# Copying softmax reciprocals to all partitions: four one-row DMA transfers in place of one four-row transfer, in a planned attention and spectral-filter kernel

## The chip, the core and the metric

The kernel runs on one core of a Trainium2 chip. The core has a matrix engine (PE, "TensorE"), a vector engine (DVE), a scalar engine (ACT, which computes exponentials), a general engine (POOL, "GpSimd") and a sequencer (SP) that here issues nearly all DMA transfers. Matrix products go to PSUM banks (512 float32 columns by 128 partitions); everything else lies in SBUF (128 partitions) or in DRAM. The metric is the device time of one launch in microseconds (us), lower is better; the median of several runs counts. The profile is of one further execution.

## The reference, cut to what matters

```
x: [1, 2048, 448]   wqkv: [448, 1344]   wo: [448, 448]   16 heads of 28
q, k, v = split(x @ wqkv)
a = softmax(q k^T / sqrt(28)) v, heads joined, @ wo
b = irfft2(rfft2(x) * (w_r + i w_i))          # over positions and channels, to bf16
g = sigmoid(sum(x * gate_w))                  # one number per position
out = g * a + (1 - g) * b
```

All inputs are bf16. The large part is the softmax: 16 heads x 2048 x 2048 = 67 million exponentials.

## The kernel before, in words

**Tiling.** Heads are taken four at a time: group g (0 to 3) has four heads, each on 32 of the 128 partitions. Queries are cut into four chunks c of 512. So there are 16 rounds n = (g, c), in an order that `plan_steps` gives (line 676). In each round the 2048 keys are 16 tiles kt of 128. A unit is one head's score tile, 128 keys by 512 queries.

**Exact exponentials.** Scores go to the PSUM tiles psA (three units) and psB (two units) in turn; ACT takes the exponential of all three or two at once (line 1307) into a ring of 28 slots in SBUF. These are the 336 steps of the kernel. A product with v (`pvb<-ring,vw`) sums over keys into one PSUM bank, and the same product sums the weights, so that row 28 of each head's 32 partitions has the softmax's denominator.

**Approximated exponentials.** `ND[n]` of the 16 key tiles of a round don't go through ACT: DVE adds a constant to the score and writes it as a 16-bit integer that read as bf16 is roughly an exponential (line 1261, four per key tile), three copies shifted by a fraction of an octave are made on POOL or DVE (line 1273), and four products with v (`pvb<-pd,vd`) average the error away. Their scores go to one of two shared PSUM banks, bg.

**Background.** The same two banks also serve the projections of q and k, v, and the Fourier part. The latter has a forward half (`fwd`, `fwd2`, each tile copied by a DMA, `xtok<-Ab`), a middle half that multiplies by the weights (loads `CS` and `Wg`), and a last part of 16 tiles, for each of which SP reads `V<-xtok` and `og<-gsc`, PE multiplies (`bg<-A,V`) and DVE writes X (line 1678). Output tiles (`out_tile`, `last_tile`) add the Fourier part (`bg<-Bd,X`) and the attention part (`bg<-wo,q`) in PSUM.

**Normalisation.** At the end of a round, `normalise` (line 1396) copies the PSUM bank to pvs (DVE, line 1443), SP moves the four rows of denominators to a 128 x 16 tile (`rs<-pvs`), DVE takes reciprocals (line 1446), POOL multiplies by the gate (line 1447), SP writes them to a DRAM scratch of four rows of 512 (`rsc<-rrg`), SP copies each of the four rows to 32 partitions (`Rb<-rsc`), and POOL multiplies pvs by Rb into q's place (line 1456). The last round does this with PE and no DMA.

**What sets the order.** The program order of each engine is written out by a planner. `Sched.run` simulates the engines with a guessed duration for each operation and a guessed latency for each hand-over, takes at each moment the ready operation with the smallest key, and emits the instructions in that order. Keys are due times: of the step that needs a result, minus a lead. The engines then run in the planned order, each waiting on semaphores for what it needs, so a late transfer stops the engine that awaits it and all that is planned behind. The constants that the change touches are these. `ND` is the number of approximated key tiles per round. `LRB` and `LREM` are planned latencies of the Rb copy and of the two Fourier copies (added to an issue's duration). `TA, TB` are the time span over which the Fourier part is due, `WREL` how long before its due time its forward half may start. `FLEAD`, `XLEAD`, `QLEAD`, `WLEAD`, `PJE` and `PJV` are leads and spreads of the projections. `DUE_P`, `DHOLD`, `PLEAD`, `EL`, `ELAST` place the approximated exponentials, `PVD` their products with v, `URG` and `DUP` are priorities on PE, `SWP` a penalty for a change of PE's tiling, `RWAIT` how long PE is kept free for a score, `KO` and `KP` the delay of output tiles and the lead of the last partial sums.

```
T.append(t)                                   # plan_steps, l. 709: start of a step
t += 0.052 + 512 * len(st) / 1200.0
def due(c): return t_a + (t_b - t_a) * c / total          # background, l. 1554
d = self.dma(lambda v2=v2: v2[:], ..., vev + [v2r[t % 2]], k - 4, lat=LREM)   # V<-xtok, l. 1663
```

Of the kernel before, what the change touches and what calls it, by code (L numbers as in the profile page):

```python
# [31 lines left out]
def free_dims(ap, dims, offset=0):  # L32
    return _AP(tensor=ap.tensor, offset=ap.offset + offset,
               ap=[list(ap.ap[0])] + [list(d) for d in dims])


def rows_of(ap, row0, stride, count, dims, offset=0):
    pitch = ap.ap[0][0]
    return _AP(tensor=ap.tensor, offset=ap.offset + row0 * pitch + offset,
               ap=[[pitch * stride, count]] + [list(d) for d in dims])  # L40
# [133 lines left out]
FIRST = 0  # L174
FWANT = (0.4, 0.45, 0.5, 0.55)
HAND = 0.15
DUE_P = 4.97
SWP = 0.58
PVA, PVD = -2, 0.69
URG = 1  # L180
FLEAD = 3.91
SQPOOL = 0
EL, ELAST = 1.87, 2
NLD = 2
KP = 26.63
KN, KO, PLEAD, DSP, DHOLD, RWAIT, WREL, XLEAD, QLEAD, WLEAD = 0, 19.35, 3.2, 0.49, 6.47, 1.51, 18.58, 8.27, 12.54, 4.09
DW, DS = 0.64, 0.4
LDMA, LREM, LRB = 2.02, 3.04, 6.5
DUP = 0.55


def frees(o):
# [3 lines left out]
class Sched:  # L196
# [60 lines left out]
    def run(self, nbg_tiles, dunits, dfree):  # L257
# [94 lines left out]
        while left:  # L352
            progress = False
            for e in engs:
# [8 lines left out]
                for o in pend[e]:  # L363
# [4 lines left out]
                    if o.acq is not None:  # L368
                        bl = [b for b in range(nbg_tiles) if held[b] is None and banks[b] <= t + 1e-9]
                        if not bl:  # L370
                            continue
                        if ud is not None and o.name != "dunit" and len(bl) == 1 and ud < o.key + DUP:
                            continue
# [3 lines left out]
                    if e == "PE":  # L377
                        if o.name == "pv" and URG and any(o in exps[i].deps for i in range(nexte, nexte + URG) if i in exps):
                            k -= 60.0
                        sw = SWITCH if (mode is not None and o.mode is not None and mode != o.mode) else 0.0  # L380
                        if sw:
                            k += SWP
                        if o.name != "score" and nexts in scores:
# [141 lines left out]


class Kernel:
    ND = [0, 3, 3, 3, 3, 3, 3, 4, 3, 3, 3, 3, 3, 2, 3, 4]
    RING = 28
    T0 = 10.0  # L530
    PJE, PJV = 25.21, 16.0
    TA, TB = 46.46, 360.74

    def __init__(self, ctx, tc, A_x, A_wqkv, A_wo, w_r, w_i, gate_w, out):
        self.ctx, self.tc, self.nc = ctx, tc, tc.nc
# [139 lines left out]
    def plan_steps(self):  # L675
# [5 lines left out]
        for n, (g, c) in enumerate(self.groups):  # L681
            nd = self.ND[n]
            dk = [NT - 1 - i for i in range(nd)]
# [503 lines left out]
    def attention(self):  # L1187
# [7 lines left out]
        for b in range(4):  # L1195
            due = ts[0] + 4 * b * rate
            if b:
                self.x_block(b, due - XLEAD)
                self.proj_fast(b, due - FLEAD)
            wop = self.w_block(0, [b], due + 5.0)  # L1200
# [31 lines left out]
        for n, kt in dlist:  # L1232
# [15 lines left out]
            for s in range(4):  # L1248
                it = Item()

                def fm(s=s, g=g, c=c, kt=kt, it=it):
                    self.mm(self.bgi(it), self.k[g][32 * s:32 * s + 32, 128 * kt:128 * kt + 128],
                            self.q[g][32 * s:32 * s + 32, 512 * c:512 * c + 512], True, True, tile_position=(32 * s, 0))
                due = fdue[0] - DUE_P + DSP * s
                m = sc.op("PE", 0.22, fm, self.kev[g, kt // 4] + self.qev[g, c], due - 1, rel, "row", it, name="dunit")
# [140 lines left out]
    def normalise(self, n, last):  # L1396
        nc, sc = self.nc, self.sc
        g, c = self.groups[n]
        i = n % 2
        t0 = self.tstart[n + 1] + 2.0  # L1400
        if not hasattr(self, "nlast"):
            self.nlast, self.rblast = [None, None], None
        pvs, rs, rr, rrg = self.pvs[i], self.rs[i], self.rr[i], self.rrg[i]
        dst = self.q[g][:, 512 * c:512 * c + 512]
        if n == 15:
            kk = -50.0
            ev = []
            for h in range(2):
                ev.append(self.act(0.33, lambda h=h: self.pin(nc.scalar.copy(
                    out=pvs[:, 256 * h:256 * h + 256], in_=self.pv[:, 256 * h:256 * h + 256])),  # L1410
                    last + [self.nlast[i]] + ev, -100.0))
            sums = self.psA[:, 2, :]
            home = [self.pv[:], self.psA[:, 1, :]]
            ms = []
            for j in range(4):
                ms.append(self.pe(0, lambda j=j: self.mm(sums[:, 4 * j:4 * j + 4], pvs[:, 128 * j:128 * j + 128],
                                                         self.c("self").bitcast(F32)[:, 0:128:32], True, True),
                                  [ev[j // 2], self.lastexp[0]] + ms[-1:], kk, dur=0.25))
            r = self.rs[i]
            a = self.dve(0.2, lambda: self.pin(nc.vector.reciprocal(out=r[:], in_=sums[:, 0:16])), ms[-1:], kk)  # L1420
            self.lastrec = a
            xs = []
            for h in range(2):
                xs.append(self.dve(0.3, lambda h=h: self.pin(nc.vector.tensor_tensor(
                    out=self.Rx[:, 2 * h:2 * h + 2, :].rearrange("p j (s n) -> p j s n", n=32),
                    in0=free_dims(r[:], [[4, 2], [1, 4], [0, 32]], 8 * h),
                    in1=free_dims(self.glog[:], [[1, 2], [0, 4], [0, 32]], 12 + 2 * h), op=ALU.mult)),
                    [a, self.gate_f32, self.rblast] + xs, kk, lk=True))
            ms2 = []
            for j in range(4):  # L1430
                ms2.append(self.pe(0, lambda j=j: self.mm(home[j // 2][:, 128 * (j % 2):128 * (j % 2) + 128],
                                                          self.Rx[:, j, :], self.c("idf").bitcast(F32), True, True),
                                   [xs[j // 2]] + ev[1:] + ms2[-1:], kk, dur=0.25))
            self.onlast = []
            for j in range(2):
                self.onlast += [self.dve(0.37, lambda j=j: self.pin(nc.vector.tensor_tensor(
                    out=dst[:, 256 * j:256 * j + 256], in0=pvs[:, 256 * j:256 * j + 256],
                    in1=home[j][:, 0:256], op=ALU.mult)), [ms2[2 * j + 1], ev[1]], kk + j)] * 2
            for t in range(12, 16):
                self.last_tile(t)  # L1440
            return ev[1]
        kk = t0 + KN
        ev = self.dve(0.61, lambda: self.pin(nc.vector.tensor_copy(out=pvs[:], in_=self.pv[:])),
                      last + [self.nlast[i]], -100.0)
        d1 = self.dma(lambda: rs[:], lambda: rows_of(pvs[:], DH, 32, 4, [[16, 32], [1, 16]]), (ev,), kk)
        a = self.dve(0.16, lambda: self.pin(nc.vector.reciprocal(out=rr[:], in_=rs[:])), (d1,), kk)
        b = self.pool(0.15, lambda: self.pin(nc.gpsimd.tensor_tensor(out=rrg[:], in0=rr[:], in1=self.G4[:, c, :],
                                                                     op=ALU.mult)), [a] + self.g4d, kk)
        sc_ = self.rsc[i]
        d2 = self.dma(lambda: sc_[:].rearrange("s (r j) -> (s r) j", j=16), lambda: rrg[:], (b, self.nlast[i]), kk, dur=DS)  # L1450

        def bc():
            src = sc_[:]
            return _AP(tensor=src.tensor, offset=src.offset, ap=[[512, 4], [0, 32], [1, 512]])
        ds = [self.dma(lambda: self.Rb[:], bc, (d2, self.rblast), kk, dur=0.55, lat=LRB)]
        e = self.pool(1.15, lambda: self.pin(nc.gpsimd.tensor_tensor(out=dst, in0=pvs[:], in1=self.Rb[:], op=ALU.mult)),  # L1456
                      ds, kk)
        self.nlast[i] = self.rblast = e
        self.onorm[g, c] = e
        if g == 3:  # L1460
            for t in range(4 * c, 4 * c + 4):
                self.out_tile(t, t0 + KO)
        return ev
# [36 lines left out]
    def last_tile(self, t):  # L1500
# [7 lines left out]
        if t % 2:  # L1508
            k0 = 6
            itp = Item()  # L1510
            part = self.sq[:].bitcast(F32)[:, 512 * (i // 2):512 * (i // 2) + D]
            kp = self.tstart[16] - KP + i
            ps = []
# [216 lines left out]
```

## Time and profile before

| | |
|---|---|
| median of 3 runs | 407.27 us (407.16 to 408.46) |
| profiled execution | 407.7 us, of which the span from first to last instruction 405.9 us |
| ACT busy | 386.7 us (95%) |
| PE busy | 383.3 us (94%), mean granted clock 0.992 |
| DVE, POOL busy | 290.7 us (72%), 247.5 us (61%) |
| DMA | 20.93 MB in 30271 packets, mean 52 GB/s |
| Rb<-rsc | 15 transfers of 256 KB, issued from 57.2 to 382.7 us, 547 ns for an issue |
| V<-xtok | 16 transfers of 112.5 KB, issued from 312.2 to 364.2 us |

How to read it: a group names its line, engine and operation, then what it writes and reads (`ring<-psA`), how often it ran, the busy time of all and the mean of one, and after a second bar the engine's idle time before it with who ended it. A matmul's line is that of a helper (L669), and a DMA issue's too (L644), so those are told apart by their tiles. In a timeline a line has the start, the length, the engine and the operation, with an idle time in square brackets. The granted clock is the share of full speed that PE was given.

### The profile page before, as it was taken

What the parts mean: (1) busy time and instruction counts of PE and PEld (TensorE: products, weight loads), DVE (VectorE), ACT (ScalarE), POOL (GpSimd) and SP (SyncE); (2) the same over time, 40 slices, a digit from 0 to 9 for tenths busy, and PEclk for the clock granted to TensorE, in tenths of its full rate; (3) what the DMA queues carried; (4) which work ended last, traced back from release to release, by engine and by line L of the source; (5) the groups of instructions that cost most, each with busy time, mean ns of one, the idle gap of its engine ahead of it and who ended that gap; (6) DMA issues with size and microseconds to landing.
All of it is one profiled execution on the core that took longest, in us unless ns stands there. A gap on an engine that the chain in (4) does not pass through costs nothing.

```text
span 405.9 us, 14400 instructions
## 1 busy us (share of the span) xinstructions
PE 383.3 (94%) x6206; PEld 154.3 (38%) x6207; DVE 290.7 (72%) x502; ACT 386.7 (95%) x355; POOL 247.5 (61%) x226
## 2 busy tenths in 40 slices
PE   8999999999999999999999999999998999979996
PEld 5444333334433333333443333444343334323333
DVE  1654776788787978977889888788677567544782
ACT  3999999999999999999999999999999999988992
POOL 8811583571656579389596895677797953353310
PEclk9999999999999999999999999999999999988999
DMA  8600012100101131121211221121211122220111
GB/s 204 161 2 5 7 45 55 47 25 18 41 26 47 49 82 60 32 64 28 57 45 38 56 52 42 40 77 30 68 30 47 46 84 71 66 80 14 38 39 45
DMA packets 30271, 20.93 MB, mean 52 GB/s; under 512 B 15508, under 2 KB 28032, under 8 KB 30208
## 3 DMA queue, kind: packets, MB, share of 16 engines
q1 hardware_dynamic: 29440, 19.70, 17.6%
q8 instruction: 48, 0.79, 0.8%
q10 hardware_dynamic: 768, 0.32, 0.4%
q14 instruction: 15, 0.12, 0.1%
HBM read 14.13 MB, written 1.97 MB: 40 GB/s over the span
## 4 chain that ended last, share of the span: by engine, by line
ACT 65%; PE 21%; issue 10%; DMA 3%; DVE 0%; ACTq 0%
ACT ring L1307 65%; PE bg L669 7%; PE pvb L669 5%; PE psA L669 4%; PE psB L669 3%; DMA V<-xtok 1%; DMA xtok<-in_A_x_dram 1%; PE bg L672 1%; DVE vw L1140 0%; DVE V L1537 0%; ACT w L1089 0%; PE psB L672 0%; PE pvb L672 0%; ACT ge L1159 0%; ACTq L1307 0%
## 5 line engine op out<-in xcount | busy, mean ns | idle before, releaser
L1307 ACT ACTIVATE ring<-psA 128x1536 bf16<-128x1536 f32 x168 | 275.5, 1640 | 5.8 <-PE psA L669 5.6
L1273 POOL TENSOR_SCALAR pd<-pd 128x2048 uint16<-128x2048 uint16 x99 | 186.0, 1902 | 71.2 <-DVE pd L1261 45.3
L1307 ACT ACTIVATE ring<-psB 128x1024 bf16<-128x1024 f32 x168 | 204.3, 1216 | 0.4 <-PE bg L669 0.4
L1261 DVE TENSOR_SCALAR pd<-bg 128x512 uint16<-128x512 f32 x184 | 124.7, 686 | 40.5 <-PE bg L669 37.9
L669 PEld LDWEIGHTS <-k 32*128 32x128 bf16 x1024 | 46.7, 91 | 126.3 <-issue 118.6
L669 PE MATMUL pvb<-ring,vw 128*32 128x512 bf16 x840 | 77.9, 386 | 0.0
L669 PE MATMUL psA<-q,k 32*128 32x512 bf16 x504 | 66.8, 384 | 10.2 <-ACT ring L1307 6.9
L669 PE MATMUL bg<-q,k 32*128 32x512 bf16 x184 | 70.4, 385 | 0.0
L669 PE MATMUL psB<-q,k 32*128 32x512 bf16 x336 | 65.9, 383 | 4.2 <-ACT ring L1307 3.3
L669 PE MATMUL pvb<-pd,vd 128*32 128x512 bf16 x736 | 67.4, 384 | 0.0
L1456 POOL TENSOR_TENSOR q<-pvs,Rb 128x512 bf16<-128x512 f32 x15 | 19.1, 1274 | 22.8 <-DVE pd L1273 21.2
L669 PEld LDWEIGHTS <-vw 128*32 128x32 bf16 x840 | 20.4, 95 | 27.3 <-issue 24.1
L669 PEld LDWEIGHTS <-vd 128*32 128x32 bf16 x736 | 19.4, 95 | 20.1 <-issue 15.0
L1273 DVE TENSOR_SCALAR pd<-pd 128x2048 uint16<-128x2048 uint16 x39 | 26.5, 703 | 0.4
L669 PEld LDWEIGHTS <-xT 128*32 128x32 bf16 (+1 forms) x1280 | 20.1, 96 | 11.8 <-issue 8.9
L1629 DVE TENSOR_TENSOR t<-bg,Wg 128x450 bf16<-128x450 f32 x32 | 18.8, 617 | 4.1 <-PE bg L669 2.2
L669 PE MATMUL bg<-xT,wpq 128*32 128x512 bf16 (+2 forms) x243 | 19.2, 383 | 0.1
L669 PE MATMUL bg<-xT,wpk 128*32 128x512 bf16 (+2 forms) x244 | 18.6, 380 | 0.0
L669 PE MATMUL bg<-Bd,xT 128*32 128x450 bf16 (+1 forms) x256 | 17.5, 357 | 0.0
L669 PE MATMUL bg<-Bd,X 113*32 113x448 bf16 x240 | 17.0, 370 | 0.3 <-DVE X L1678 0.3
L669 PE MATMUL bg<-wo,q 128*32 128x448 bf16 x232 | 16.3, 363 | 0.0
L1575 DVE CAST X<-bg 128x450 bf16<-128x450 f32 x16 | 10.0, 625 | 8.7 <-PE bg L669 8.4
(119 smaller groups left out, 351.0 us busy)
## 6 DMA issues: line engine op xcount, KB each, us to landing
Rb<-rsc SPq DMA_DIRECT2D x15, 256.0 KB
CS<-cCS SPq DMA_DIRECT2D x16, 192.0 KB
xtok<-Ab SPq DMA_DIRECT2D x16, 112.5 KB
V<-xtok SPq DMA_DIRECT2D x16, 112.5 KB
xtok<-in_A_x_dram SPq DMA_DIRECT2D x4, 448.0 KB
out_dram<-fin SPq DMA_DIRECT2D x12, 112.0 KB
Wg<-in_B_w_r_dram SPq DMA_DIRECT2D x32, 28.1 KB
Wg<-in_B_w_i_dram SPq DMA_DIRECT2D x32, 28.1 KB
```

The costliest lines, as they stand in the source:

```text
L669: self.pin(self.nc.tensor.matmul(out, lhsT=lhsT, rhs=rhs, start=start, stop=stop, **kw))
L672: self.pin(self.nc.tensor.transpose(out=out, in_=in_, identity=self.c("ident")[0:n, 0:n]))
L1261: self.pin(nc.vector.tensor_scalar(out=ys[:, s, :].bitcast(U16), in0=self.bgi(it), scalar1=127 * UNITS, scalar2=0.0, op0=ALU.add, op1=ALU. ...
L1273: self.pin(e.tensor_scalar(out=fl(pds), in0=fl(ys), scalar1=float(PHASE[f]), scalar2=1.0, op0=ALU.add, op1=ALU.mult))
L1307: self.pin(nc.scalar.activation(out=self.ring[:, u0:u0 + len(st), :], in_=slot[:, 0:len(st), :], func=ACT.Exp, scale=LN2 / UNITS))
L1456: e = self.pool(1.15, lambda: self.pin(nc.gpsimd.tensor_tensor(out=dst, in0=pvs[:], in1=self.Rb[:], op=ALU.mult)), ds, kk)
L1575: x1.append(self.dve(.54, lambda: self.pin(nc.vector.tensor_copy(out=self.X1[:, t, 0:F2], in_=self.bgi(it)[:, 0:F2])), ops[-1:] + pads, k, ...
L1629: self.pin(nc.vector.tensor_tensor(out=out[:], in0=self.bgi(it)[:, 0:F2].rearrange("p (a f) -> p a f", a=2), in1=free_dims(Wg[:], [[F - 2 ...
```

## The change

The copy of the reciprocals, one DMA whose source has three dimensions (four rows, each read 32 times, 512 numbers), becomes four DMAs, one per row, each to its own 32 partitions. The planner counts each with 0.5 us of issue and the latency LRB. The multiply on POOL depends on all four. Beside it 22 constants and the list ND have new values. The rest of the planner and all arithmetic stay.

```diff
-DUE_P = 4.97
-SWP = 0.58
-PVA, PVD = -2, 0.69
-URG = 1
-FLEAD = 3.91
+DUE_P = 7.01
+SWP = 0.98
+PVA, PVD = -2, 0.64
+URG = 2
+FLEAD = 6.57
 SQPOOL = 0
-EL, ELAST = 1.87, 2
+EL, ELAST = 1.93, 2.4
 NLD = 2
-KP = 26.63
-KN, KO, PLEAD, DSP, DHOLD, RWAIT, WREL, XLEAD, QLEAD, WLEAD = 0, 19.35, 3.2, 0.49, 6.47, 1.51, 18.58, 8.27, 12.54, 4.09
+KP = 24.94
+KN, KO, PLEAD, DSP, DHOLD, RWAIT, WREL, XLEAD, QLEAD, WLEAD = 0, 20, 3.19, 0.49, 6.56, 1.49, 4, 8.32, 16.29, 5.66
 DW, DS = 0.64, 0.4
-LDMA, LREM, LRB = 2.02, 3.04, 6.5
-DUP = 0.55
+LDMA, LREM, LRB = 2.02, 3.0, 3.16
+DUP = -1.85
...
-    ND = [0, 3, 3, 3, 3, 3, 3, 4, 3, 3, 3, 3, 3, 2, 3, 4]
+    ND = [0, 3, 3, 3, 2, 3, 4, 3, 4, 3, 3, 3, 4, 1, 3, 4]
     RING = 28
     T0 = 10.0
-    PJE, PJV = 25.21, 16.0
-    TA, TB = 46.46, 360.74
+    PJE, PJV = 24.12, 18.53
+    TA, TB = 46.46, 356.48
...
-        def bc():
-            src = sc_[:]
-            return _AP(tensor=src.tensor, offset=src.offset, ap=[[512, 4], [0, 32], [1, 512]])
-        ds = [self.dma(lambda: self.Rb[:], bc, (d2, self.rblast), kk, dur=0.55, lat=LRB)]
+        ds = []
+        for k in range(4):
+            def bc(k=k):
+                src = sc_[:]
+                return _AP(tensor=src.tensor, offset=src.offset + 512 * k, ap=[[0, 32], [1, 512]])
+            ds.append(self.dma(lambda k=k: self.Rb[32 * k:32 * k + 32, :], bc, (d2, self.rblast), kk, dur=0.5, lat=LRB))
```

## The prediction

> **What bounds the kernel now.** I read the page first: the span, the busy shares, the chain that ended last.
>
> ```profile
> span 405.9 us, 14400 instructions
> PE 383.3 (94%) x6206; PEld 154.3 (38%) x6207; DVE 290.7 (72%) x502; ACT 386.7 (95%) x355; POOL 247.5 (61%) x226
> ACT 65%; PE 21%; issue 10%; DMA 3%; DVE 0%; ACTq 0%
> L1307 ACT ACTIVATE ring<-psA 128x1536 bf16<-128x1536 f32 x168 | 275.5, 1640 | 5.8 <-PE psA L669 5.6
> L1307 ACT ACTIVATE ring<-psB 128x1024 bf16<-128x1024 f32 x168 | 204.3, 1216 | 0.4 <-PE bg L669 0.4
> ```
>
> ACT is the bound: 336 exponentials, one of each kind per pair, follow each other from 10.95 to 396.29 us. Time can come only out of the places where ACT waits. By the starts in ACT's timeline the median pair lasts 2.252 us (1.640 + 1.216 would be 2.86; neighbours overlap). The last pair starts at 393.69, that is 382.74 us after the first for 167 pairs, and 167 x 2.252 = 376.1. So the stream loses 6.65 us in all. Head (10.95) and tail (405.9 - 396.29 = 9.6) are prologue and last output tiles, which the transfer isn't part of.
>
> Where are the 6.65 us? The view of stretches answers with the granted clock, here before, at and after the one bad place (columns: stretch, us, busy us of PE, PEld, DVE, ACT, POOL with counts, clock, DMA share, GB/s):
>
> ```profile
> 312.00:357.00 45.00, 43.40 (x766) 18.01 (x766) 27.74 (x46) 45.00 (x41) 25.15 (x16) 1.00 0.23 69
> 357.00:370.00 13.00, 10.43 (x140) 3.28 (x136) 5.18 (x8) 9.43 (x9) 6.86 (x4) 0.74 0.19 57
> 370.00:396.00 26.00, 25.43 (x392) 9.14 (x392) 19.05 (x31) 25.90 (x24) 7.12 (x5) 1.00 0.10 30
> ```
>
> ACT is full on both sides and idle for 3.57 us of the 13 between. ACT's timeline there, PE's first late matmul, and the chain:
>
> ```profile
> 360.18 1.71 ACT L1307 ACTIVATE ring<-psA 128x1536 bf16<-128x1536 f32 x1
> 364.81 1.45 ACT L1307 ACTIVATE ring<-psA 128x1536 bf16<-128x1536 f32 x1 [1.99 <-PE psA L669]
> 368.86 1.45 ACT L1307 ACTIVATE ring<-psA 128x1536 bf16<-128x1536 f32 x1 [1.21 <-PE psA L669]
> 371.32 1.45 ACT L1307 ACTIVATE ring<-psA 128x1536 bf16<-128x1536 f32 x1
> 363.55 0.61 PE L669 MATMUL bg<-A,V 128*32 128x128 bf16 x16 [2.55 <-DMA V<-xtok]
> 357.44 6.06 DMA V<-xtok
> ```
>
> Three pairs take 371.32 - 360.18 = 11.14 us where 3 x 2.252 = 6.76 would do: 4.38 us lost. PE, which runs in order, stood 2.55 us for a read of V (issued at 357.44, used 6.06 us later); when it went on, a four-matmul group took 0.61 instead of 0.39 us until about 369, the 0.74 of the clock column. The other 2.27 us are spread: 0.97 over the first 20 pairs, 0.1 to 0.3 per later 20.
>
> Why was V late? The DMA issues just before, the DMA rate from 357 to 363 in 40 slices of 0.15 us, and two stretches in which one transfer alone moves (Rb, then CS):
>
> ```profile
> 355.15 0.62 SPq L644 DMA_DIRECT2D V<-xtok  x1
> 355.86 0.55 SPq L644 DMA_DIRECT2D Rb<-rsc  x1
> 356.50 0.85 SPq L644 DMA_DIRECT2D og<-gsc  x1
> 357.44 0.61 SPq L644 DMA_DIRECT2D V<-xtok  x1
> ...
> GB/s 169 53 61 74 80 61 65 93 63 75 116 175 201 169 158 103 68 68 60 65 68 89 93 89 103 205 212 193 202 131 104 83 81 75 49 27 24 24 24 17
> ...
> 77.10:80.10 3.00, 3.00 (x45) 1.03 (x42) 1.43 (x3) 3.00 (x4) 3.00 (x3) 1.00 0.25 91
> 208.90:209.90 1.00, 1.00 (x16) 0.41 (x19) 0.85 (x3) 1.00 (x2) 1.00 (x2) 1.00 0.80 219
> ```
>
> Rb keeps 0.25 of 16 engines, four, busy for 3 us; CS, 128 rows in its outer dimension, keeps 0.80 busy for 1 us. Rb is 128 packets of 2 KB at 84 ns each by the packet records: 32 per engine on four engines, 2.7 us. In the last 0.6 us before 363 one engine alone still drains (24 GB/s): it had Rb's row, then the V packets. V went out behind Rb on that engine.
>
> **The change, part by part.** (1) *Four transfers.* Packets and bytes stay (128 of 2 KB). A source with 32 rows outermost can be dealt over 16 engines, eight packets on each in all: 8 x 84 ns = 0.67 us per engine, not 2.7. I take 16 by CS; the other end is that four engines stay. [...]
>
> *What it adds:* 45 issues on SP, three in each of 15 normalisations. An issue costs 0.38 us (wo<-, 28 rows) to 0.58 (rs<-); nearest is G<-gsc, 32 rows from DRAM, 0.42. With 0.05 between them, 4 x 0.42 + 3 x 0.05 = 1.83 instead of 0.55: 1.28 us later for what is behind on SP (ends: 1.1 and 1.9). SP issues for 138 us of 405.9, so only transfers directly behind matter. The multiply on POOL needs all four, but isn't late now: in all 15 cases it starts 0.9 us or more after Rb's last packet (behind pd copies, or held for DVE's pd copy: 21.2 us in all). Nothing is gained there. If it did wait, pd copies behind it on POOL would be late, 1.9 us each, and PE's pvb matmuls after them.
>
> *At the stall, in the old order:* V, now issued at 357.44, goes at 358.7. An undisturbed V ends its packets 1.95 us after issue, rs 1.54; rs is in use 2.56 after issue, so V after about 2.97: at 361.7. PE was free for it at 363.55 - 2.55 = 361.0. A wait of 0.7 is left of 2.55, and I expect no slow clock after it: PE's other waits, up to 0.50 us, had none. From V's matmuls to the psA matmuls takes 0.46 (354.71 to 355.17), from those to the exponential 0.49 (355.17 to 355.66): 362.65, where 360.18 + 2.25 = 362.43 would be on time, so 0.2 is lost. Gain 4.38 - 0.2 = 4.2 us. Ends: 0 if V is as late as now, 4.4 if the wait goes.
>
> (2) *Planned latencies* LRB 6.5 to 3.16, duration 0.55 to four of 0.5. From the first issue the planner now allows 2.0 + 3.16 = 5.16 us before the multiply; by the sum above it is 1.4 (last issue) + 1.33 (first packet) + 0.3 + 1.0 (rs, last packet to use) = 4.0. Cover 1.1 us; zero cost. LREM stays within 0.04.
>
> (3) *ND* still adds up to 46 groups of approximated exponentials: 840 units on ACT, 184 first steps on DVE and 138 copies as before. Group starts shift by one quad, 4/5 of a pair = 1.8 us, for four groups. Zero in sum.
>
> (4) *Leads and priorities.* TB 360.74 to 356.48 makes the transform's last reads due 4.3 us earlier, so fewer fall behind the Rb of group 13. FLEAD +2.7, QLEAD +3.8, WLEAD +1.6, DUE_P +2.0 pull projections and first steps ahead; WREL 18.58 to 4 holds the forward transform back, which before was already late (its first copy went out at 66.4, planned due near 56). The trace can't show a new order. Bounds: the 2.27 us of spread loss all gone, or every pair like the first 20, where projections crowd: 0.97/20 x 168 = 8.1, that is 5.8 more than now. I take zero, since the 120 pairs behind the first 20 lose only 0.011 each, in a plan with the same work.
>
> Sum against the profiled execution, 407.7 us (span 405.9 and 1.8 around it): 407.7 - 4.2 = 403.5. That execution is 0.4 above the median of 407.27, so **403.1 us**.
>
> **Rivals.** *The stall stays or moves* (no change): some read is again 2 us late, because the four still share engines with V, or an instruction fetch holds one (16 KB packets of 0.9 to 1.4 us lie through the trace). The price is one 4.4: 407.5. For it: a 1.07 us fetch at 357.1 helped here. Against: only one such wait in 385 us.
>
> *Crowding* (slower): the leads take the two bg banks and PE's slots earlier, and scores come some hundredths late in every pair. It decides when the loss per pair passes 4.2/168 = 0.025 us over today's. At the first 20 pairs' 0.048 it is 403.1 + 5.8 = 408.9. For it: PE is 94% busy. Against: the stretches from 57 to 357, where ACT stands at 100%.
>
> *Late reads through SP* (slower): 1.3 us more in front of reads that PE awaits, in a plan with 0.7 us of cover for V (3.66 planned, 2.97 real). Two waits past the length that brings the half clock (between 0.50 and 2.55 us) cost 8.8: 411.9. For it: the one that the kernel has came in this way. Against: SP idles for most of the span. [...]
>
> *It does not spread:* four transfers still on four engines; then V is as late as before, 407.3.
>
> **How the numbers follow.** Spreading with a clean order 0.48 (its own range 401.5 to 405.9); stall stays or moves 0.08, no spreading 0.04, crowding 0.25, late reads 0.15. Of the two no-change cases some 0.03 fall on either side. Faster by over 0.3% 0.51, within 0.3% (1.2 us, what a measurement here can tell) 0.06, slower 0.43. For 8 in 10 the range runs from 401.5 (nearly all 6.65 us recovered would give 400.6) up through crowding to 411.0, with about 0.15 above it and 0.05 below.
>
> **What would show it.** Right: four Rb groups of issues, 60 in all; a DMA share well over 0.25 while they move; no PE wait over 1 us on V; clock 1.00 from 57 to 390; ACT's idle before psA near 2.2 us (the head's 2.15). Wrong: pairs over 2.28 us through the middle (crowding), a new PE wait on V, CS or Wg with a clock under 0.9 behind it, or POOL idle on Rb.

## The result, and the profile after

The changed kernel takes 404.53 us (median of 6 runs, 404.05 to 405.00) against 407.38 us for the kernel before. The ratio is 0.9923, with a 95% interval from 0.9905 to 0.9941: 2.85 us faster, where 4.2 had been forecast. Its profiled execution took 405.0 us with a span of 403.2.

From the page of the changed kernel:

```profile
span 403.2 us, 14388 instructions
PE 385.4 (96%) x6166; PEld 154.0 (38%) x6167; DVE 292.5 (73%) x502; ACT 386.5 (96%) x355; POOL 247.5 (61%) x226
ACT 67%; PE 16%; issue 11%; DVE 2%; SPq 1%; DMA 1%; DVEq 0%; POOL 0%; ACTq 0%; POOLq 0%
L1307 ACT ACTIVATE ring<-psA 128x1536 bf16<-128x1536 f32 x168 | 277.1, 1649 | 2.9 <-PE psA L669 2.8
L1307 ACT ACTIVATE ring<-psB 128x1024 bf16<-128x1024 f32 x168 | 206.0, 1226 | 0.0
```

ACT's idle time before psA fell from 5.8 to 2.9 us, of which 2.15 is the wait before the very first step. The same steps in ACT's timeline, the same three stretches, and what SP issued there (the x4 line is four issues of Rb):

```profile
361.73 1.71 ACT L1307 ACTIVATE ring<-psA 128x1536 bf16<-128x1536 f32 x1
363.99 1.71 ACT L1307 ACTIVATE ring<-psA 128x1536 bf16<-128x1536 f32 x1
366.25 1.71 ACT L1307 ACTIVATE ring<-psA 128x1536 bf16<-128x1536 f32 x1
...
312.00:357.00 45.00, 44.11 (x777) 17.75 (x769) 27.67 (x45) 45.00 (x41) 25.21 (x16) 1.00 0.24 72
357.00:370.00 13.00, 12.44 (x228) 4.97 (x224) 7.89 (x12) 13.00 (x13) 9.85 (x6) 1.00 0.18 54
370.00:396.00 26.00, 25.76 (x361) 9.52 (x353) 15.71 (x26) 24.39 (x24) 4.12 (x4) 1.00 0.11 30
...
356.17 0.62 SPq L644 DMA_DIRECT2D V<-xtok  x1
356.88 0.41 SPq L644 DMA_DIRECT2D og<-gsc  x1
358.30 3.00 SPq L644 DMA_DIRECT2D Rb<-rsc  x4
361.40 1.32 SPq L644 DMA_DIRECT2D V<-xtok  x2
```

The pairs follow each other every 2.26 us, ACT is full through the stretch, and the clock is 1.00. No matmul waits for V any more; one weight load still does, for 0.2 us. But the order is another too: the read of V that used to go out behind round 13's copy now goes out ahead of it. So this profile alone doesn't tell whether the spreading or the order did it.

The span gives up 405.92 - 403.21 = 2.71 us. By the same sums as before: pairs 140 to 159 lose 0.13 instead of 4.45 (-4.32); the first 20 pairs lose 1.85 instead of 0.97 (+0.88); the other pairs 1.45 instead of 1.23 (+0.22); the first exponential starts at 11.71 instead of 10.95 (+0.76); the tail takes 9.47 instead of 9.63 (-0.16). The remaining -0.09 is in the last steps' lengths.

The +0.76 at the head is no effect of the change. PE starts slow and the clock's record of full speed begins at 4.1 us in the first profile and at 7.1 in this one: the first group of four transposes takes 0.63 us here where it took 0.40. In a second profile of the kernel before (below) full speed begins at 7.0 and the first exponential at 11.67, in a second one of the changed kernel at 5.2 and 10.98. The +0.88 belongs to the new order and came back in the second profile of the changed kernel (1.85 again): a projection of q stands ahead of the key block's transposes, and one pair takes 26.51 - 23.29 = 3.22 us. ACT, then PE:

```profile
23.29 1.46 ACT L1307 ACTIVATE ring<-psA 128x1536 bf16<-128x1536 f32 x1
26.51 1.45 ACT L1307 ACTIVATE ring<-psA 128x1536 bf16<-128x1536 f32 x1 [0.48 <-PE psA L669]
...
23.09 0.83 PE L669 MATMUL bg<-xT,wpq 128*32 128x512 bf16 x12
25.43 0.38 PE L672 MATMUL bg<-cst,k 128*128 128x128 bf16 x4 [0.30 <-DVE q L981]
25.97 0.45 PE L669 MATMUL psA<-q,k 32*128 32x512 bf16 x3
```

### The profile page after: what moved, and what is told of

Same layout as the page of the kernel before. It is cut to its first block, busy times and chain, and to the rows that moved or that the text cites. A ratio compares the mean times of both kernels' runs of the same rounds, so it can differ in the third digit from the quotient of the medians.

```text
span 403.2 us, 14388 instructions
## 1 busy us (share of the span) xinstructions
PE 385.4 (96%) x6166; PEld 154.0 (38%) x6167; DVE 292.5 (73%) x502; ACT 386.5 (96%) x355; POOL 247.5 (61%) x226
## 4 chain that ended last, share of the span: by engine, by line
ACT 67%; PE 16%; issue 11%; DVE 2%; SPq 1%; DMA 1%; DVEq 0%; POOL 0%; ACTq 0%; POOLq 0%
ACT ring L1307 67%; PE bg L669 5%; PE psA L669 5%; PE pvb L669 4%; PE psB L669 2%; SPq L644 1%; PE bg L672 1%; DMA Rb<-rsc 0%; DMA rsc<-rrg 0%; DVE q L981 0%; ACT w L1089 0%; DVE t L1631 0%; DVE sq L991 0%; DVE pd L1261 0%; DVE xtok L1655 0%
## 5 line engine op out<-in xcount | busy, mean ns | idle before, releaser
L669 PE MATMUL bg<-q,k 32*128 32x512 bf16 x184 | 69.1, 383 | 0.2 <-DVE q L981 0.2
L669 PEld LDWEIGHTS <-vd 128*32 128x32 bf16 x736 | 18.5, 95 | 19.9 <-issue 15.5
L1447 POOL TENSOR_TENSOR rrg<-rr,G 128x16 f32<-128x16 f32 x15 | 3.3, 218 | 33.9 <-DVE pd L1273 20.6
```

The source lines that it names most:

```text
L669: self.pin(self.nc.tensor.matmul(out, lhsT=lhsT, rhs=rhs, start=start, stop=stop, **kw))
```

## The experiments

### Is it the spreading? Four transfers in the old order

```diff
 (the kernel before, all constants and the written order kept)
-        ds = [self.dma(lambda: self.Rb[:], bc, (d2, self.rblast), kk, dur=0.55, lat=LRB)]
+        def emit():
+            for k in range(4):
+                self.pin(nc.sync.dma_start(out=self.Rb[32 * k:32 * k + 32, :], in_=bc(k)))
+        ds = [sc.op("SP", 0.55, emit, (d2, self.rblast), kk, 0.0, lat=LRB, name="dma")]
```

> The kernel before with its constants and its written order; only where SP issued the one copy of four rows it now issues four of one row, back to back. Theory 1, spreading: Rb leaves the four engines after 0.7 us, the read of V behind round 13's copy is in time, the half clock does not come: 4.2 us less than before, about 403.1 us, and the loss of pairs 154 to 156 (4.38 us) under 0.5. Theory 2, order and constants: the copies alone change nothing, 407.4, and the stall at 363 us stays. Theory 3, issue time: three more issues, 1.3 us, push V back as much as the spreading brings it forward: a wait of 1 to 2 us on V stays, 405 to 408.

Measured: 404.52 us, ratio 0.9932 (0.9912 to 0.9952). That is the changed kernel's time, with no constant changed. It is 1.4 us more than the 403.1 that had been expected, although the stall is gone: what is left of the loss is worked out in the part on the prediction below. SP's issues in the former stall, and whom PE waits for over the whole run (total, times, longest, in us):

```profile
356.69 0.63 SPq L644 DMA_DIRECT2D V<-xtok  x1
357.42 2.00 SPq L1458 DMA_DIRECT2D Rb<-rsc  x4
359.51 0.91 SPq L644 DMA_DIRECT2D og<-gsc  x1
360.46 0.63 SPq L644 DMA_DIRECT2D V<-xtok  x1
...
PE bg L669 <- DMA xtok<-Ab: 1.0, 1, 1.0
PE bg L669 <- DMA V<-xtok: 0.5, 1, 0.5
```

Here the read of V still goes out behind the copies, at 360.46, 3.0 us behind the first of them where it was 1.6, and yet PE waits 0.5 us instead of 2.55 and the clock stays at 1.00. The spreading is enough by itself.

### Is it the order? One transfer in the new order

```diff
 (the changed kernel, all constants and the written order kept)
+        def emit(k):
+            if k == 0:
+                self.pin(nc.sync.dma_start(out=self.Rb[:], in_=bc()))    # one copy of four rows
+        ds = [sc.op("SP", 0.5, lambda k=k: emit(k), ..., lat=LRB, name="dma") for k in range(4)]
```

> The changed kernel with its constants and its written order; only the four copies are one copy of four rows again, issued where the first of them was, so SP has 45 issues fewer. Theory 1, spreading: the two reads of V that follow round 13's copy (361.4 us) wait behind it on its engines, the wait and the half clock come back: 407 to 409 us. Theory 2, order and constants: the new order keeps the reads clear of the copy anyway: 404.5 us, within 0.3%. Theory 3, issue time: fewer issues, no harm: 404.0 us or less.

Measured: 405.46 us, ratio 0.9950 (0.9929 to 0.9971). None of the three theories gave this. PE waits for V again, but for 1.25 us, and no half clock follows:

```profile
PE bg L669 <- DMA V<-xtok: 1.2, 1, 1.2
```

So the new order alone saves 1.75 us (407.21 to 405.46): it moves one read of V out of the copy's way, and pairs 140 to 159 lose 1.22 us where they lost 4.45. The four transfers in it are worth about another 1 us: 0.9 between medians, whose intervals overlap, and 1.1 in these pairs by the profiles (0.13 against 1.22). The gain of the new order and that of the four transfers don't add up, since both remove the same stall.

### Is it round 13's copy? Leaving it out

```diff
 (the kernel before)
+        def emit():
+            if n != 13:
+                self.pin(nc.sync.dma_start(out=self.Rb[:], in_=bc()))
```

> The kernel before, with the copy of round 13 alone left out (that round multiplies by round 12's reciprocals, so one chunk of one group of heads is wrongly scaled); the order is kept. If the copy of this round is the cause of the late read of V: no wait on V over 0.5 us, no half clock, 403.0 us, 4.4 less. If the fetch of instructions at 357.1 us or the other reads are: V still late by 1 to 2 us and 405.5 to 407.4 us.

Measured: 404.08 us, ratio 0.9920 (0.9902 to 0.9939), no wait on V, no half clock. One copy of 15 caused the stall. It also bounds the gain: without that copy at all it is 3.1 us between medians, not the 4.4 that had been expected.

### How long is the stall? The kernel before once more

The kernel is unchanged, so there is no edit.

> The kernel before, unchanged, profiled a second time. The first profile lost 4.38 us in pairs 154 to 156, but leaving out round 13's copy gained only 3.1 us between medians. Theory A, the first profile was an execution with a long stall: the loss at these pairs is now 2 to 3.5 us, or the span is within 1 us of 404.8. Theory B, the stall is 4.4 us in every execution and leaving the copy out costs 1 us elsewhere: 4.2 to 4.5 us again.

Measured, in one execution: 407.54 us, span 405.8. Its ACT timeline and its stretch:

```profile
360.90 1.71 ACT L1307 ACTIVATE ring<-psA 128x1536 bf16<-128x1536 f32 x1
365.17 1.45 ACT L1307 ACTIVATE ring<-psA 128x1536 bf16<-128x1536 f32 x1 [1.63 <-PE psA L669]
368.90 1.45 ACT L1307 ACTIVATE ring<-psA 128x1536 bf16<-128x1536 f32 x1 [1.20 <-PE psA L669]
371.15 1.46 ACT L1307 ACTIVATE ring<-psA 128x1536 bf16<-128x1536 f32 x1
...
357.00:370.00 13.00, 10.36 (x166) 3.57 (x168) 5.37 (x8) 10.11 (x9) 6.87 (x4) 0.87 0.21 64
```

The same three pairs lose 371.15 - 360.90 - 6.76 = 3.49 us instead of 4.38. PE's wait for V was as long (2.61 us), but the half clock lasted 3.4 us instead of 6.8: the mean clock of these 13 us is 0.87 instead of 0.74, which is 3.4 and 6.8 us at half speed. Theory A holds, though at the upper end of its 2 to 3.5 us.

The runs' mean clocks say how often each case comes. One stretch of 3.4 us at half clock takes 0.004 off the mean of a run. Of 46 further executions of the kernel before, on three chips, 25 have 0.995 or 0.996 as the second profile has, 17 have 0.992 or 0.993 as the first has, three 0.989 and one 0.999. On each chip the ones at 0.992 or 0.993 took 0.5 to 1.0 us longer on average than those at 0.995 or 0.996. So the first profile showed the dearer and less frequent case.

### Fewer engines: two transfers of two rows

```diff
 (the kernel before, order kept)
+            return _AP(tensor=src.tensor, offset=src.offset + 512 * 2 * k, ap=[[512, 2], [0, 32], [1, 512]])
+            for k in range(2):
+                self.pin(nc.sync.dma_start(out=self.Rb[64 * k:64 * k + 64, :], in_=bc(k)))
```

> The kernel before with its order; the copy is two transfers of two rows each, back to back. Theory 1, spreading (engines are as many as the outermost dimension has rows): two engines carry all 128 packets, 64 each, 5.4 us of 84 ns packets instead of 2.7; the DMA share while Rb moves alone is 0.12, V comes 2 to 3 us later than before, the multiply on POOL begins to wait, 409 to 413 us. Theory 3, number of transfers: two do half of what four do, 405 us. If the engines are shared out in another way (two times four): as before or better, 405 to 407 us.

Measured: 421.79 us, ratio 1.0331 (1.0275 to 1.0386), far above the 409 to 413 that had been expected. Three waits of PE, of 2.38, 3.06 and 4.07 us, each come with a half clock, 23.9 us of it in all. A stretch in which the two transfers move, who POOL's multiply waits for, and PE's waits for V; then, for comparison, a stretch in which the changed kernel's four move:

```profile
84.00:90.20 6.20, 6.20 (x90) 1.94 (x79) 4.29 (x8) 6.20 (x7) 5.06 (x3) 1.00 0.13 44
POOL q L1460 <- DMA Rb<-rsc: 31.7, 8, 10.3
PE bg L669 <- DMA V<-xtok: 7.8, 3, 4.1
PE psA L669 <- DMA q<-nrow: 2.4, 1, 2.4
```
```profile
129.40:131.40 2.00, 2.00 (x30) 0.63 (x27) 1.31 (x3) 2.00 (x3) 0.85 (x1) 1.00 0.40 131
```

The DMA share is 0.13 of 16 engines (two) at 44 GB/s, 0.25 (four) at 91 for the one transfer before, and 0.40 at 131 for four transfers. Two rows outermost take two engines although the transfers are twice as many, and the copies then last 5.7 to 6.6 us. In these runs the share followed the rows outermost in the source, and with 32 rows it passed that of four engines. In the packet records of these stretches at most 3 packets of the two transfers are under way at once, 6 of the one and 14 of the four. The 0.40 doesn't count the engines, since the issues set the pace: they are 0.46 us apart, and 128 packets of 84 ns over 16 engines in 4 x 0.46 us would be a share of 0.36 (an estimate). One transfer with many rows outermost was not tried.

### What an issue costs: eight transfers of 16 rows

```diff
 (as the four in the old order)
-            for k in range(4):
-                self.pin(nc.sync.dma_start(out=self.Rb[32 * k:32 * k + 32, :], in_=bc(k)))
+            for k in range(8):
+                self.pin(nc.sync.dma_start(out=self.Rb[16 * k:16 * k + 16, :], in_=bc(k)))
```

> As the four transfers in the old order, but eight of 16 rows each, back to back. The engines stay 16, the issues double: 3.8 us on SP instead of 2.0. Theory 1 with issue time: V goes out 1.8 us later than with four, PE waits 2 to 2.5 us for it instead of 0.5, and whether the half clock comes decides between 406 and 408 us. Theory that only the engines count: 404.5 us as with four.

Measured: 409.31 us, ratio 1.0048 (1.0023 to 1.0073). SP needed 5.06 us for round 13's eight (3.8 expected), PE stood 3.05 us where 2 to 2.5 had been expected, and the time is above the 406 to 408 of the expectation:

```profile
357.45 5.06 SPq L1458 DMA_DIRECT2D Rb<-rsc  x8
363.07 0.62 SPq L644 DMA_DIRECT2D V<-xtok  x1
365.63 0.40 PE L669 MATMUL bg<-A,V 128*32 128x128 bf16 x16 [3.05 <-DMA V<-xtok]
```

So the price of issues is real and ends the gain between four and eight pieces of this copy. With eight pieces of 32 KB the trace shows as the reason the read of V, which waits behind them in SP's queue: it goes out 5.62 us after the first of them, where it was 3.04 with four.

### Four transfers, planned anew with the old constants

```diff
 (the kernel before, all constants kept, LRB 6.5 too; the planner writes a new order)
-        ds = [self.dma(lambda: self.Rb[:], bc, (d2, self.rblast), kk, dur=0.55, lat=LRB)]
+        ds = []
+        for k in range(4):
+            def bc(k=k): ...                # row k, 32 times
+            ds.append(self.dma(lambda k=k: self.Rb[32 * k:32 * k + 32, :], bc, (d2, self.rblast), kk, dur=0.5, lat=LRB))
```

> The kernel before with all its constants (LRB 6.5 too), but the planner counts four issues of 0.5 us, as the diff has it: the first part of the change alone. The order is written anew. Theory 1, spreading is what pays and constants do not: 404.5 us within 1 us. Theory 2, the constants had to be searched for the four transfers: 406 us or more, with a new wait of PE or a spread loss over 3 us in the stream.

Measured: 409.65 us, ratio 1.0042 (1.0031 to 1.0053): slower than before, and 4.5 to 5 us slower than the same four transfers in the old order (by the ratios, 1.0042 against 0.9932, and by the medians, which are of two chips). The spreading is there and PE doesn't wait for V. The time is in two other places that the new order made, a wait for a ring slot at 125 us and the tail:

```profile
127.32 1.02 ACT L1307 ACTIVATE ring<-psB 128x1024 bf16<-128x1024 f32 x1 [2.04 <-PE pvb L669]
398.29 0.65 ACT L1409 COPY pvs<-pvb 128x256 f32<-128x256 f32 x2 [2.90 <-issue]
```

One pair takes 4.58 us, and from the last exponential to the end it takes 12.96 us instead of 9.63. Why the tail is longer in this order isn't shown.

### One constant at a time

```diff
 (four transfers, replanned, old constants)
-LDMA, LREM, LRB = 2.02, 3.04, 6.5
+LDMA, LREM, LRB = 2.02, 3.04, 3.16
```

> The kernel before with four planned issues and one constant of the change, LRB 6.5 to 3.16; all other constants old. With LRB 6.5 this was 409.65 us, from a wait on a ring slot at 125 us (2.3) and a tail of 13.0 us instead of 9.6. Theory, LRB is the constant that the four transfers need: both go, 405 us. Theory, the constants act together and any one of them only draws another order: another set of waits, 405 to 411, with the loss at other places.

Measured: 407.76 us, ratio 1.0004 (0.9994 to 1.0015), no difference from the kernel before. The tail is 10.3 us, the wait at 125 us is gone, and there is one at 88 us instead:

```profile
ACT ring L1307 <- PE psB L669: 2.4, 1, 2.4
```

And the other way, the changed kernel with one constant back:

```diff
-... XLEAD, QLEAD, WLEAD = ... 8.32, 16.29, 5.66
+... XLEAD, QLEAD, WLEAD = ... 8.32, 12.54, 5.66
```

> The changed kernel with one constant back, QLEAD 16.29 to 12.54. In the changed kernel the fifth pair behind the start lasts 3.23 us instead of 2.25, where a projection of q stands in front of the key block's transposes on PE. Theory crowding by that lead: the fifth pair is back at 2.3 us and the first 20 pairs lose 0.9 us instead of 1.85, total 403.6 us if the rest of the order holds. Theory that another lead (FLEAD, XLEAD) does it: 3.2 us again and 404.5.

Measured: 410.05 us, ratio 1.0058 (1.0037 to 1.0079). The pair at 23 us is back at its length, as expected, but the first 20 lose 1.34 us (0.9 expected) and the time is 6.4 us above the 403.6 expected. The order behind it is another one, with a pair of 6.04 us at 240.6, again a wait for a ring slot:

```profile
245.67 1.03 ACT L1307 ACTIVATE ring<-psB 128x1024 bf16<-128x1024 f32 x1 [3.40 <-PE pvb L669]
```

A constant can't be judged alone here: each draws another order, and three orders drawn in this way cost 3 to 6 us more than the two best.

### Are the constants worth anything? Both on one chip

The four transfers in the old order, and the changed kernel, both as they were.

> The four transfers in the old order once more, beside the changed kernel on the same chip. Theory, the constants only keep what the spreading gives: the same time as the changed kernel within 0.3%, 404.5 us. Rival, the searched constants are worth something of their own: the changed kernel is faster by 1 us or more.

> The changed kernel once more, for the comparison with the four transfers in the old order: 404.5 us by the theory that the constants add nothing, and its profile again with the pair at 23 us 1 us too long and no wait of PE on V.

Measured: 404.32 us, ratio 0.9929 (0.9910 to 0.9949), and 404.30 us, ratio 0.9923 (0.9910 to 0.9937). No difference. The second profile of the changed kernel has the long pair again, 3.23 us at 22.6, and no matmul that waits for V; that of the four in the old order has a wait of 0.98 us on V, where the first had 0.5, and no half clock.

### Can the rest be had? Copies behind the read of V

```diff
 (the four in the old order; round 13's are held back)
+            if t == 13:                     # the next read of V
+                def both(first=d.emit):
+                    first()
+                    self.held13()           # the four issues of round 13
+                d.emit = both
```

> The four transfers in the old order; round 13's four are issued behind the next read of V instead of ahead of it. The multiply that needs them has 3 us to spare. Theory, the wait of 0.5 us on V that is left comes from the issue time: it goes, 404.0 us, no more than 0.5 us gained. Rival, other transfers hold V: 404.5 as before.

Measured: 404.04 us, ratio 0.9920 (0.9904 to 0.9935). The wait on V is gone, so it did come from the issues. The time is the lowest median of all, but its interval covers the 404.3 of its neighbours: nothing that can be told from them. A version that clearly beats the changed kernel was not found.

## Why the prediction was right, and where it was off

**Right: the place and the mechanism.** The one late read of V behind round 13's copy was what could be gained; leaving that copy out gains 3.1 us between medians, and no run gained more than that by an amount that can be told. That four rows keep to four engines (a share of 0.25) is confirmed by two rows, which keep to two (0.13). That 32 rows are dealt over all 16 was the author's estimate, and no run shows it: the share was 0.40, with at most 14 packets under way at once. The half clock doesn't come with the wait that is left: 0.7 us had been forecast, 0.5 was measured, 0.98 in a second run. For the four issues 1.83 us had been worked out. Most groups of four took 1.7 us, but round 13's took 2.00 and 2.98 in the two profiles of the old order, and 3.00 and 2.33 in those of the changed kernel.

**Off: the size of the stall, 4.38 us.** The forecast of 4.2 us gained failed in that term. It was taken from one execution. A second one lost 3.49 at the same place with the same wait, because the half clock behind it was half as long, and between medians the copy costs 3.1. The sum used one execution's price, of the dearer case, against a median. By the second profile, 3.5 less the 0.2 that was taken for the leftover wait makes 3.3, against the measured 2.85. The sums over the stream account for the rest. Against that second profile, whose first exponential starts at nearly the same time (11.67 and 11.71), the changed kernel's span is 2.54 us shorter: pairs 140 to 159 lose 3.41 less, the last steps and the tail take 0.27 less, and the other pairs lose 1.10 more, of which 0.88 is the new order's in the first 20. The old order with four transfers hasn't got that 0.88 and yet took the same time, because it loses elsewhere: in its two profiles pairs 60 to 79 lose 1.07 and 0.68 us where the changed kernel loses 0.25, at a wait that is named at the end, and pairs 140 to 159 lose 0.21 and 0.54 where it loses 0.13. In all its stream loses 3.30 and 3.14 us, that of the changed kernel 3.44 in both of its profiles.

**Off: part 4, the leads at zero.** They cost 0.88 us in the first 20 pairs (the rival of crowding, at a sixth of its price and in one pair only, not in all). Against the four transfers in the old order they come out at zero all the same, 404.30 against 404.32, since the new order also has no wait on V or on the copied tiles. That is luck rather than the reason given, which was that the plan does the same work.

**Half right: "zero cost" for the planned latencies and the list ND.** In the order that the searched constants give they cost nothing that shows. But the step treated the four planned issues as a change of timing, and they are a change of order: with the old constants that order costs 4.5 to 5 us (409.65 against 404.52). This was neither in the sum nor among the rivals. What the constants were needed for is to get back what the replanning took.

**Rivals.** Late reads through SP: it exists, at eight transfers (3.05 us of wait, 409.31); at four in the old order 0.5 to 0.98 us of wait are left, without a half clock. Crowding: seen at 23 us, small. No spreading: refuted by the DMA shares, 0.40 against 0.25. The stall moves: not in the changed kernel; with one transfer in the new order 1.25 us of it stayed.

**A sign that misled.** The prediction named POOL idle on Rb as a mark of failure. In the first profile of the changed kernel POOL's multiply waits for Rb twice, 7.3 us together. In the second the same two multiplies stand as long, but the long wait, 6.3 us, is put down to PE, and only 0.9 us to Rb. The stream loses 3.44 us in both, and no pair near these waits is long, so no cost of it shows.

## What to carry to other kernels

A transfer that is off the critical path can still hold one that is on it, as this copy held a read of V that PE then awaited for 2.55 us. Look at how many DMA engines it uses (share of 16 while it moves alone: here 0.13 with two rows outermost, 0.25 with four, 0.40 with 32), and try an outermost dimension of more rows, in few issues: here four transfers came to 0.9932 of the time before, eight to 1.0048. Price a stall from more than one execution when a slow clock follows it, since the clock's part varied here (3.4 and 6.8 us). And where a planner writes the order, compare an edit in the old order and in the new one separately: here the edit was worth 2.7 to 3.3 us in the old order, and with the old constants the new order more than took that back.

## What the runs showed of the hardware

*The half clock, a granted clock of 0.50, lasted 3.4 us, or two or four times that.* In the fourteen profiles, between the head and the tail, it came with PE waits of 2.38 us and more (2.38, 2.55, 2.61, 3.05, 3.06, 4.07) and never with one of 1.28 or less (0.95, 0.98, 1.15, 1.25, 1.28); no wait lay between. It didn't start at a fixed point: in the first profile of before at 362.53, inside the wait from 361.00 to 363.55, in the second at 365.41, 1.1 us after the wait had ended. It lasted 3.4 us in the second profile of before and with eight transfers, 6.8 in the first profile of before, and 13.7, 6.8 and 3.4 in the run with two. What sets its start and its length isn't shown. One of the 46 executions of the kernel before that have no profile shows no such stretch at all (mean clock 0.999, 406.07 us); whether its read of V came in time or its wait brought no half clock isn't known.

*A long issue on SP nearly always met an instruction packet: 127 of 130.* In the fourteen profiles 130 DMA issues on SP after the first 12 us took over 0.85 us, where most take 0.3 to 0.7, and 127 of them overlap a 16 KB packet of the queue that the profile calls instruction. The reverse doesn't hold: 452 shorter issues overlap one too. The third of round 13's four in the changed kernel is a long one: 1.70 us from 359.14, with a packet from 358.93 for 1.54 us. It is why that group took 3.00 us where most take 1.7. The kernel before has 7 such issues, the changed kernel 14 and 12, the eight transfers 15, but the four in the old order 7 again, so more issues don't always meet more packets. That the packet is what holds the issue wasn't tried.

*A read of the same plan was late in some runs and not in others.* PE waits near 168 us for 0.6 to 1.3 us before `bg<-xtok,CS` in four of the runs in the old order (the profile names `xtok<-Ab` as the one waited for in two of them) and not in three others. The order of instructions up to there is the same in the kernel before, which hasn't got the wait, and in the one without round 13's copy, which has. Its cause stays open.
